# Attention and top-1 mixture of experts on one Trainium2 core: small list copies on another engine, second weight matrix loaded whole, smaller descriptor scratch

## The chip, the cores and the metric

The kernel runs on one core of one Trainium2 chip. The metric is the time of one execution in device microseconds (us); runs are summed up by their median.

## The reference

There is an attention with a sigmoid in place of the softmax, and then a mixture of experts in which each token goes to one expert.

```python
scores = scale * np.matmul(q, k.transpose(0, 1, 3, 2)) - np.log(S)      # 8 x 12 heads, 448 tokens, 64 wide
attn = np.matmul(1.0 / (1.0 + np.exp(-scores)), v)
x = attn laid out as 3584 tokens x 768
logits = x @ w_gate; e_idx = argmax(logits); gate_w = softmax(logits)[e_idx]
eom = sigmoid(x @ w_output_gate)
for e in range(8):
    h = np.maximum(x[mask] @ w1[e], 0.0)      # w1: 768 x 1024
    out[mask] = gate_w * eom[:, e] * (h @ w2[e])      # w2: 1024 x 768
```

## The kernel before, in words

**The stages.** Up to about 269 us the kernel computes the attention on TensorE (PE), writes the token rows to `x_dram` and finds the expert of each token. The mixture follows as a row of *slots*. A slot holds tokens of one expert: 11 full slots of up to 256 tokens (33.3 us each, the first from 272.6 us), then 3 wide slots of up to 192 (27.5 us each, `wide_slot`, from 640.9 us), then 2 half slots of up to 128 (`half_slot`, from 725.3 us to the end). How many of each kind run is read from a table at run time. Every slot after the first full ones stands inside an If on these counts (L1066 full, L1071 wide, L1076 and L1079 half), one nested in the other, so that after the last wide slot one If is not taken and all engines jump out to the half slots.

**One slot.** PE multiplies x by w1 (`layer1`, L623 and L624 in full slots, L797 to L799 in half slots) and the result h by w2 (`layer2`, L648 to L650). Each fp32 operand is split into a rounded high part and a remainder, and three products are added up. The splits are the work of two engines: ScalarE (ACT) writes the high part (L579 for w2 and x, L583 for w1), VectorE (DVE) the remainder (L580, L586). In `half_slot` ACT does, in this order: the high part of w2 rows 0 and 1, then of rows 2 and 3 (both L579), relu of the first half of h (L803), the high part of rows 4 and 5 (L805), a split of h (L579), the high part of rows 6 and 7 (L795), relu of the second half of h (L803). PE's `turn` (L782) transposes each half of h; it comes once in the middle of layer 1 and once after the first part of layer 2.

**What is fetched for the next slots.** GpSimd (POOL) gathers the x rows of the slot after the next, eight transfers per full slot (L545), by the row numbers in a list; DVE transposes them (`turn_x`, L605). SyncE (SP) loads the weights of the next slot as three transfers of w1 and four of w2 (L566), each of two "rows" of 128 x 768 or 128 x 1024 elements. A load is issued only once the engines that read the old content are done.

**The lists.** Row numbers, output rows and gates of a slot are spread from 32 partitions over 128 by small copies, 12 in each of `spread_lists` (L505, L507, L508; five calls) and `spread_two` (L518, L521; two calls), 8 in `spread_rest` (L530, L531; one call): 92 instructions, all on POOL. Before them DVE transposes the list (L501, L513). Two calls lie in the attention (221 and 259 us), one in the second full slot, one in the third, and `spread_two`, two `spread_lists` and `spread_rest` in the fourth one (372.6 to 406.0 us, the code calls it m = EARLY). POOL executes its queue in order: in that slot copies, gathers, the sending of results (L670) and a `drain` (L696) stand in one line.

**w2 in the wide slots.** A wide slot loads only rows 0 to 3 of the next slot's w2 at its end (`load_w2(nx, (0, 2))`). It copies the expert's number and the flag into the tile `held` (L764, DVE). The slot that follows begins with `load_held` (L736 in a wide slot, L770 in the first half slot): SP reads `held` into registers (L539) and issues the loads of rows 4 and 5 and of rows 6 and 7.

Of the kernel before, what the change touches and what calls it, by code (L numbers as in the profile page):

```python
# [42 lines left out]
LATE_F = LATE_MAX + 2  # L43
LATE_N = LATE_F + E + 2
GT = 32
LGR = LATE_N // 4
# [8 lines left out]
def r32(ap):  # L55
    return ap.bitcast(F32)


class Kernel:
# [80 lines left out]
    def constants(self):  # L140
        nc = self.nc
# [64 lines left out]
        own = gl[1].bitcast(I32)  # L206
        a = TS
# [10 lines left out]
        self.ltb = own[:, a:a + 2 * E].rearrange("p (k h w) -> p k h w", h=1, w=2)  # L218
        a += 2 * E
        self.at = own[0:GT, a:a + LGR + 1]  # L220
        a += LGR + 1
        self.held = own[0:1, a:a + 2]

    def row_words(self):
        v, tok = self.nc.vector, self.tok
# [181 lines left out]
    def table_late(self):  # L407
        v = self.nc.vector
# [9 lines left out]
        first = self.tmp_off  # L418
# [61 lines left out]
        v.tensor_copy(self.tab_l[:, 0], both(0)[0:1])  # L480
        v.tensor_copy(self.tab_b, T[0:1, :, 2, 0:E])
        v.tensor_copy(self.tot, end[0:1, :, E - 1])
        v.memset(self.held, 0)
        yield 1

    def take(self, key, tiles):
# [11 lines left out]
    def spread_lists(self, raw, lt, lx):  # L498
        nc, k, g = self.nc, lx.shape[1], lx.shape[2]
        t = self.take("lt32", self.lt32)  # L500
        nc.vector.transpose(t, raw.rearrange("p (t w) -> p w t", w=6))  # L501
        copy = nc.gpsimd.tensor_copy
        for i in range(4):
            r = slice(32 * i, 32 * i + 32)
            copy(lx[r], t[:, i, 0:k * g].rearrange("p (k g) -> p k g", g=g))  # L505
            own = t[:, :, 0:k * g].rearrange("p w (k h q) -> p w k h q", k=k, q=4)
            copy(lt[r, :, :, 0], own[:, 4, :, :, i])  # L507
            copy(r32(lt[r, :, :, 1]), own[:, 5, :, :, i])  # L508

    def spread_two(self, raw, lt, lx):  # L510
        nc, t = self.nc, self.lt32_two
        for j in range(2):
            nc.vector.transpose(t[:, j], raw[:, Q4 * j:Q4 * j + Q4].rearrange("p (t w) -> p w t", w=6))  # L513
        copy = nc.gpsimd.tensor_copy
        two = lambda a: a.rearrange("p (j k) g -> p j k g", j=2)
        for i in range(4):
            r = slice(32 * i, 32 * i + 32)
            copy(two(lx[r]), t[:, :, i].rearrange("p j (k g) -> p j k g", g=8))  # L518
            for w in range(2):
                to = lt[r, :, :, w]  # L520
                copy(two(r32(to) if w else to),  # L521
                     t[:, :, 4 + w].rearrange("p j (k h q) -> p j k h q", h=2, q=4)[:, :, :, :, i])

    def spread_rest(self):
        g = self.nc.gpsimd
        a = EARLY + LATE_F
        for i in range(4):
            r, q = slice(32 * i, 32 * i + 32), slice(32 * (i % 2), 32 * (i % 2) + 32)
            own = self.lts[q, a:, 1]
            g.tensor_scalar(self.ltq[r, :, 0], own[:, :, 0], 2.0, float(i // 2), ALU.mult, ALU.add)  # L530
            g.tensor_copy(r32(self.ltq[r, :, 1]), r32(own[:, :, 1]))  # L531
# [39 lines left out]
    def load_w2(self, s, rows=range(0, 8, 2)):  # L571
        if s is not None:
            self.load_w(s, self.w2, self.w2r, rows)

    def load_held(self):
        self.load_w2(self.slot_regs(self.held.unsqueeze(2), 0, 1), (4, 6))

    def split(self, raw, hi, lo):
        self.nc.scalar.copy(hi, raw)  # L579
# [152 lines left out]

    def wide_slot(self, j, hint):
        cur = self.wide_lists(j)
        if j:
            self.load_held()  # L736
        nx = self.load_slot(self.tab_l, LATE_F + j + 1, self.wide_lists(j + 1))
        self.nc.gpsimd.drain()
        self.split_w2(0)
        for f in range(8):  # L740
            if f == 6:
                self.finish()
            self.layer1(f, n=WS)
            if f == 0:
                hint()
            if f:
                self.high_low(f - 1, HS)
            if f in (1, 3, 5):
                self.split_w2(f // 2 + 1)
        self.high_low(7, HS)  # L750
        self.high_w1(0)
        self.turn_x(nx)
        self.gather(self.wide_lists(j + 2))
        for k in range(3):
            self.split_x(nx, k)
        self.low_w1(0)
        self.split_w1(1)
        self.split_w1(2)
        self.layer2_q(cur, self.ys[0])
        self.load_w2(nx, (0, 2))  # L760
        self.layer2(cur, 0, 0, self.ys[1], self.psy[1])
        self.layer2_due(cur, 0)
        k = LATE_F + j + 1
        self.nc.vector.tensor_copy(self.held, self.tab_l[0:1, 0:3:2, k])  # L764

    def half_slot(self, j, y):
        nc = self.nc
        nx = None
        if j == 0:
            self.load_held()  # L770
        if j + 1 < E:
            nx = self.load_slot(self.tab_b, j + 1, self.half_lists(j + 1))
        if j:
            if nx is not None:
                self.gather(self.half_lists(j + 1))
            nc.gpsimd.drain()  # L776
        (wh, wl), (xh, xl), (hh, hl) = self.w1s, self.xs, self.hs

        def turn(n):
            ps = self.take("x", self.psx).rearrange("p a (b t) -> p (a b) t", b=2)  # L780
            for i in range(4):
                nc.tensor.transpose(ps[:, i], self.hb[:, 128 * (4 * n + i):128 * (4 * n + i + 1)], self.ident)  # L782
            fs = slice(4 * n, 4 * n + 4)
            self.split(ps, hh[:, fs, 0:HS], hl[:, fs, 0:HS])

        w2 = [self.w2_rows(k) for k in range(4)]
        low = lambda k: nc.vector.tensor_tensor(w2[k][2], w2[k][0], r32(w2[k][1]), ALU.subtract)
        for n in range(2):
            c = slice(512 * n, 512 * n + 512)
            ps = self.take("h", self.psh)  # L790
            for d in range(6):
                if n == 1 and d == 3:
                    turn(0)
                    low(2)
                    nc.scalar.copy(w2[3][1], w2[3][0])  # L795
                    low(3)
                nc.tensor.matmul(ps, xh[:, d, 0:HS], wh[d][:, c], start=(d == 0), stop=False)  # L797
                nc.tensor.matmul(ps, xh[:, d, 0:HS], wl[d][:, c], start=False, stop=False)
                nc.tensor.matmul(ps, xl[:, d, 0:HS], wh[d][:, c], start=False, stop=(d == 5))  # L799
            if n == 0:  # L800
                self.split_w2(0)
                self.split_w2(1)
            nc.scalar.activation(self.hb[:, c], ps, AF.Relu)  # L803
            if n == 0:
                nc.scalar.copy(w2[2][1], w2[2][0])  # L805
        cur = dict(lt=self.ltb[:, j])
        pss = self.psy[0:2]
        self.layer2_mm(pss[0], 0, 0, range(2))
        turn(1)
        if j == 0:  # L810
            self.finish()
        if nx is not None:
            self.turn_x(nx)
            self.split_w1(0)
            for k in range(3):
                self.split_x(nx, k)
            self.split_w1(1)
        self.layer2_mm(pss[0], 0, 0, range(2, 4))
        self.layer2_mm(pss[1], 0, 1, range(4))
        self.load_w2(nx)  # L820
        if nx is not None:
            self.split_w1_row(4)
        for n in range(2):
            self.layer2_mm(pss[n], 0, n, range(4, 8))
            self.layer2_out(pss[n], cur, 0, n, y)
        if nx is not None:
            self.split_w1_row(5)
# [296 lines left out]
```

## Time and profile before

| what | us |
|---|---|
| median of 3 runs | 770.81 (770.23 to 771.84) |
| profiled execution, its own time | 771.06 |
| span in its profile | 769.2 |
| mean granted clock of PE in it | 0.997 of full speed |

The profiled execution lies 0.25 us over the median, and its time is 1.9 us more than the span. In the profile a line such as L566 is a line of the kernel; PE is TensorE, PEld its weight load, DVE VectorE, ACT ScalarE, POOL GpSimd, SP SyncE, and a q behind a name is that engine's sequencer. Times in rows are counted from the start of the span. `[1.24 <-DVE due L658]` says that the engine was idle for 1.24 us before the instruction and that the wait was ended by the instruction of DVE on line 658. "x3" is a count of instructions drawn together in one row. PE's matmuls overlap: one starts every 0.17 us (384 columns), 0.23 us (512) or 0.12 us (256), though each lasts longer, so a loss on PE shows as a wider distance between two starts.

### The profile page before, as it was taken

Reading aid. Unit: us, or ns where it says so; the run is one execution under the profiler, and the core shown is the slowest. Engines: PE = TensorE matmul, PEld = TensorE weight load, DVE = VectorE, ACT = ScalarE, POOL = GpSimd, SP = SyncE. Lnnn points to the kernel's source line nnn. Section 1 sums busy time; section 2 is a strip of 40 time slices with the busy share of each in tenths; the row PEclk is TensorE's granted clock in tenths of the full one; section 3 lists DMA queues with packets and bytes.
Section 4 is the critical chain, followed back from the end, with each engine's and each line's share of the span. In section 5 each row is a group of like instructions: output and inputs, shape, how many; then the busy total and the mean of one; then the engine's idle time right before and its main releaser. Section 6 shows DMA issues by size and latency. Waiting matters only on the chain. (4 is left out here: it accounts for less than half of the span.)

```text
span 769.2 us, 15280 instructions
## 1 busy us (share of the span) xinstructions
PE 756.5 (98%) x5823; PEld 581.5 (76%) x5823; DVE 493.9 (64%) x846; ACT 488.4 (63%) x654; POOL 338.0 (44%) x393
## 2 busy tenths in 40 slices
PE   9999999999999999999999999999999999999996
PEld 4457754444434389899998989999899999889785
DVE  3333345435476679967786676858577685887787
ACT  5666656666687756566665565756556574675685
POOL 5000003232154555787885647355372633633522
PEclk9999999999999999999999999999999999999998
DMA  7464544536486340256766497511156755497691
GB/s 257 145 216 138 203 164 146 159 131 217 145 319 246 122 162 1 80 202 221 260 229 225 170 322 287 157 52 41 42 218 212 268 159 215 145 351 255 224 397 47
DMA packets 43790, 145.21 MB, mean 189 GB/s; under 512 B 5671, under 2 KB 7951, under 8 KB 42672
## 3 DMA queue, kind: packets, MB, share of 16 engines
q1 hardware_dynamic: 33872, 119.56, 43.9%
q0 software_dynamic: 9824, 24.46, 9.4%
q8 instruction: 50, 0.82, 0.4%
q14 instruction: 44, 0.36, 0.1%
HBM read 152.61 MB, written 23.06 MB: 228 GB/s over the span
## 5 line engine op out<-in xcount | busy, mean ns | idle before, releaser
L623 PE MATMUL ps<-rounded 128*128 128x512 f32 (+1 forms) x672 | 226.2, 386 | 1.1 <-PEq L1066 0.8
L871 ACT ACTIVATE a<-ps,bias_s 128x896 f32<-128x896 f32 x168 | 169.0, 1008 | 87.1 <-PE ps L869 87.0
L545 POOL DMA_INDIRECT plain<-x_dram,lxs x122 | 180.4, 1479 | 67.9 <-issue 32.2
L869 PE MATMUL ps<-kqv 64*64 64x448 f32 x1344 | 194.3, 542 | 0.0
L878 PE MATMUL ps<-a,kqv 64*64 64x448 f32 x1344 | 192.4, 536 | 0.0
L624 PE MATMUL ps<-rounded 128*128 128x256 f32 (+1 forms) x672 | 184.1, 274 | 1.2 <-DVE due L658 1.2
L648 PE MATMUL ps<-w2h,h 128*128 128x384 f32 x432 | 145.0, 336 | 0.0
L580 DVE TENSOR_TENSOR w2l<-plain,w2h 128x1536 fp32r<-128x1536 f32 x60 | 105.3, 1757 | 61.9 <-ACT w2h L579 61.9
L650 PE MATMUL ps<-w2h,h 128*128 128x384 f32 x432 | 144.5, 334 | 0.0
L649 PE MATMUL ps<-w2l,h 128*128 128x384 f32 x432 | 144.5, 334 | 0.0
L623 PEld LDWEIGHTS ps<-rounded 128*128 128x128 f32 x672 | 125.9, 187 | 24.3 <-issue 2.0
L624 PEld LDWEIGHTS ps<-rounded 128*128 128x128 f32 x672 | 127.3, 189 | 1.6 <-DVE rounded L586 1.6
L869 PEld LDWEIGHTS ps<-kqv 64*64 64x64 f32 x1344 | 66.3, 134 | 67.2 <-issue 52.9
L878 PEld LDWEIGHTS ps<-a,kqv 64*64 64x64 f32 x1344 | 67.5, 133 | 60.8 <-issue 51.9
L586 DVE TENSOR_TENSOR rounded<-plain,rounded 128x2048 fp32r<-128x2048 f32 x46 | 103.4, 2286 | 2.6 <-ACT rounded L583 2.6
L631 ACT COPY gl<-ps 128x256 f32<-128x256 f32 (+1 forms) x112 | 40.4, 361 | 95.3 <-PE ps L624 89.4
L579 ACT CAST w2h<-plain 128x1536 fp32r<-128x1536 f32 x60 | 88.0, 1470 | 16.6 <-PE ps L914 4.8
L583 ACT CAST rounded<-plain 128x2048 fp32r<-128x2048 f32 x46 | 87.2, 1902 | 0.0
L648 PEld LDWEIGHTS ps<-w2h,h 128*128 128x128 f32 x432 | 81.1, 188 | 2.4 <-issue 1.8
L649 PEld LDWEIGHTS ps<-w2l,h 128*128 128x128 f32 x432 | 81.2, 188 | 0.1
L650 PEld LDWEIGHTS ps<-w2h,h 128*128 128x128 f32 x432 | 81.1, 188 | 0.0
L670 POOL DMA_INDIRECT out<-y,due x11 | 18.2, 1651 | 114.2 <-ACT gl L631 92.8
(257 smaller groups left out, 685.0 us busy)
## 6 DMA issues: line engine op xcount, KB each, us to landing
plain<-w SPq DMA_DIRECT2D x68, 768.0 KB
plain<-w SPq DMA_DIRECT2D x48, 1024.0 KB
kqv<-kqv SPq DMA_DIRECT2D x23, 1344.0 KB
x_dram<-xt SPq DMA_DIRECT2D x8, 1344.0 KB
plain<-w SPq DMA_DIRECT2D x6, 512.0 KB
plain<-x_dram,lxs POOLq DMA_INDIRECT x122, 4.3
kqv<-kqv SPq DMA_DIRECT2D x2, 448.0 KB
lst<-plain POOLq DMA_DIRECT2D x1, 726.0 KB, 6.8
```

What stands on the lines that cost most here:

```text
L545: self.nc.gpsimd.indirect_dma_start(out=s["xg"][:, g], out_offset=None, in_=x4, in_offset=bass.IndirectOffsetOnAxis(ap=s["lx"][:, g:g + 1] ...
L579: self.nc.scalar.copy(hi, raw)
L580: self.nc.vector.tensor_tensor(lo, raw, r32(hi), ALU.subtract)
L586: self.nc.vector.tensor_tensor(self.w1p[1][k], self.w1r[:, 2 * k:2 * k + 2], r32(self.w1p[0][k]), ALU.subtract)
L623: nc.tensor.matmul(out, wh[d][:, c], both, start=(d == 0), stop=False)
L624: nc.tensor.matmul(ps[:, 0:n], wl[d][:, c], self.xc[:, d, 0, 0:n], start=False, stop=(d == 5))
L648: nc.tensor.matmul(ps, hh[:, f, tk], wh, start=(f == 0), stop=False)
L649: nc.tensor.matmul(ps, hh[:, f, tk], wl, start=False, stop=False)
L650: nc.tensor.matmul(ps, hl[:, f, tk], wh, start=False, stop=(f == 7))
L869: nc.tensor.matmul(ps[half[h], j, 0:S], kg[half[j], e, 1, o:o + 64], kg[half[j], e, 0], start=True, stop=True)
L871: nc.scalar.activation(at[u % 4], ps[:, :, 0:S], AF.Sigmoid, bias=self.bias_s, scale=1.0 / math.sqrt(D))
L878: nc.tensor.matmul(self.ps_o[e][h][half[j], 0:S], v[half[h], 6 if i == 3 else 3 * e + c, j], a[half[h], j], start=(i in ((0, 3 if h else 4 ...
```

## The change

1. The 92 copies of `spread_lists`, `spread_two` and `spread_rest` are issued on DVE in place of POOL.
2. A wide slot loads all of the next w2 at its end. For rows 4 and 5, and again for rows 6 and 7, DVE first copies one element of the destination onto itself, and the load stands behind this copy. `held`, its two writes and `load_held` go.
3. The scratch for the descriptors of GpSimd's transfers is 8192 in place of 16384 bytes per partition.

```diff
@@ class Kernel
-        a += LGR + 1
-        self.held = own[0:1, a:a + 2]
...
-        v.memset(self.held, 0)
...
     def spread_lists(self, raw, lt, lx):
-        copy = nc.gpsimd.tensor_copy
+        copy = nc.vector.tensor_copy
     def spread_two(self, raw, lt, lx):
-        copy = nc.gpsimd.tensor_copy
+        copy = nc.vector.tensor_copy
     def spread_rest(self):
-        g = self.nc.gpsimd
+        g = self.nc.vector
...
-    def load_held(self):
-        self.load_w2(self.slot_regs(self.held.unsqueeze(2), 0, 1), (4, 6))
...
     def wide_slot(self, j, hint):
         cur = self.wide_lists(j)
-        if j:
-            self.load_held()
...
         self.load_w2(nx, (0, 2))
         self.layer2(cur, 0, 0, self.ys[1], self.psy[1])
         self.layer2_due(cur, 0)
-        k = LATE_F + j + 1
-        self.nc.vector.tensor_copy(self.held, self.tab_l[0:1, 0:3:2, k])
+        for q in (4, 6):
+            first = self.w2r[0:1, q, 0:1]
+            self.nc.vector.tensor_copy(first, first)
+            self.load_w2(nx, (q,))
 
     def half_slot(self, j, y):
-        if j == 0:
-            self.load_held()
...
-    nc = bacc.Bacc("TRN2", target_bir_lowering=False, num_devices=1)
+    nc = bacc.Bacc("TRN2", target_bir_lowering=False, num_devices=1, dynamic_dma_scratch_size=8192)
```

## Rows read from the trace of the kernel before

**Rows 1.** Part 1 of the page: busy time and share of the span of each engine
```profile
PE 756.5 (98%) x5823; PEld 581.5 (76%) x5823; DVE 493.9 (64%) x846; ACT 488.4 (63%) x654; POOL 338.0 (44%) x393
```

**Rows 2.** Waits of PE: waiting line, releaser, us in total, times, longest
```profile
PE ps L624 <- DVE due L658: 1.2, 1, 1.2
...
PE ps L782 <- ACT hb L803: 1.2, 1, 1.2
...
PE ps L797 <- PEq L1071: 0.7, 1, 0.7
PE ps L623 <- DVE gl L632: 0.3, 1, 0.3
```

**Rows 3.** Timeline of PE around 441 us: start, us, instruction, idle before
```profile
440.74 0.40 PE L623 MATMUL ps<-rounded 128*128 128x512 f32 x1
442.37 0.39 PE L624 MATMUL ps<-rounded 128*128 128x256 f32 x1 [1.24 <-DVE due L658]
```

**Rows 4.** Timeline of DVE in the fifth to seventh full slot
```profile
431.35 1.78 DVE L605 STREAM_TRANSPOSE plain<-plain 128x1536 f32<-128x1536 f32 x1 [6.77 <-DMA plain<-x_dram,lxs]
...
442.24 0.15 DVE L658 COPY due<-lts 128x1 int32<-128x1 int32 x1
442.30 0.14 DVE L659 COPY due<-lts 128x1 f32<-128x1 f32 x1
...
492.97 1.78 DVE L605 STREAM_TRANSPOSE plain<-plain 128x1536 f32<-128x1536 f32 x1
```

**Rows 5.** Timeline of POOL in the fourth to sixth full slot
```profile
373.05 1.00 POOL L545 DMA_INDIRECT plain<-x_dram,lxs  x1 [0.15 <-issue]
...
400.73 2.25 POOL L508 COPY lts<-wg 32x8 f32<-32x8 f32 x1
...
416.55 1.04 POOL L545 DMA_INDIRECT plain<-x_dram,lxs  x1 [8.03 <-DVE h L637]
...
461.72 0.98 POOL L545 DMA_INDIRECT plain<-x_dram,lxs  x1 [3.12 <-DVE plain L605]
```

**Rows 6.** Chain that ended last, 723 to 735 us: start, us, what
```profile
723.72 0.28 SPq L539
...
725.61 0.40 SPq L566
...
726.64 7.71 DMA plain<-w
```

**Rows 7.** Timeline of ACT in the first half slot
```profile
724.84 2.86 ACT L579 CAST w2h<-plain 128x1536 fp32r<-128x1536 f32 x2 [3.71 <-PEq L1071]
729.71 0.60 ACT L803 ACTIVATE hb<-ps 128x512 f32<-128x512 f32 x1 [2.01 <-PE ps L799]
730.50 1.48 ACT L805 CAST w2h<-plain 128x1536 fp32r<-128x1536 f32 x1 [0.20 <-DMA plain<-w]
732.24 0.59 ACT L579 CAST h<-ps 128x512 fp32r<-128x512 f32 x1 [0.26 <-PE ps L782]
...
735.81 0.59 ACT L803 ACTIVATE hb<-ps 128x512 f32<-128x512 f32 x1
```

**Rows 8.** Timeline of PE in the first half slot
```profile
731.55 0.60 PE L782 MATMUL ps<-ident,hb 128*128 128x128 f32 x4
...
736.46 0.66 PE L782 MATMUL ps<-ident,hb 128*128 128x128 f32 x4 [1.19 <-ACT hb L803]
```

**Rows 9.** Waits of DVE: waiting line, releaser, us in total, times, longest
```profile
DVE w2l L580 <- ACT w2h L579: 61.9, 50, 5.1
```

**Rows 10.** Part 5, POOL's gathers (busy, mean ns); part 6, their us to landing
```profile
L545 POOL DMA_INDIRECT plain<-x_dram,lxs x122 | 180.4, 1479 | 67.9 <-issue 32.2
...
plain<-x_dram,lxs POOLq DMA_INDIRECT x122, 4.3
```

**Rows 11.** Line 1071 (the If around the wide slots): instructions on SP's sequencer
```profile
L1071 SPq EVENT_SEMAPHORE  x9: 17/17/17, 718.8 to 721.0; - x9
```

**Rows 12.** Waits of SP: waiting line, releaser, us in total, times, longest
```profile
SPq L1071 <- SPq L1071: 6.4, 2, 4.8
```

**Rows 13.** Stretch of the first half slot: busy us of each engine, PE clock, DMA share, GB/s
```profile
731.00:738.00 7.00, 5.81 (x34) 4.95 (x33) 4.29 (x4) 4.33 (x6) 0.00 (x0) 1.00 1.03 414
```

## The prediction

> **What bounds the kernel now.** The first view is the table of busy times: PE is busy for 756.5 of 769.2 us [rows 1]. The other engines stand at 64% or less, so a change pays only where PE waits, and costs only where PE is made to wait. The second view is the list of PE's waits [rows 2], which is short. Three entries lie where this change works: 1.2 us before a matmul of L624, put down to DVE; 1.2 us before `turn` (L782), put down to ACT's relu; 0.7 us at L1071, where the wide slots are left. An entry of 0.3 us at L632 lies beside small DVE work that the change doesn't touch. The change can therefore give back about 2.7 us and no more.
>
> The third view is the timeline around the first entry. Two matmuls that usually start 0.23 us apart start at 440.74 and 442.37 [rows 3]: 1.63 - 0.23 = 1.40 us lost. DVE had finished its last w1 remainder just before L658 at 442.24 [rows 4]. It was late because `turn_x` (L605) waited 6.77 us for gathered x rows and began at 431.35 [rows 4]. In an undisturbed slot L605 comes 20.3 us after the slot's start (492.97, no wait [rows 4], the slot having begun at 472.6), which in the slot from 406.0 would be 426.3. The rows came late because POOL began that slot's gathers at 416.55 [rows 5]; an undisturbed slot begins them 22.4 us after its start (461.72 [rows 5] in the slot from 439.3), here in the slot before, at 372.6 + 22.4 = 395.0. What kept POOL were the list copies, some at 2.25 us each [rows 5], and the drain behind them.
>
> The fourth view is the chain that ended last: it goes through SP's reading of `held` at 723.72, the issues at 725.61 and 726.64, and 7.71 us to the landing of w2 rows 6 and 7 at 734.35 [rows 6]. ACT rounds them, does the second relu at 735.81 [rows 7], and `turn(1)` starts at 736.46 after 1.19 us of PE idle [rows 8]. With the distance of 0.17 us that belongs there, the loss is about 1.36 us.
>
> **Part 1, copies on DVE.** POOL loses 92 instructions; in the slot from 372.6 us it loses 44 (12 + 12 + 12 + 8). Its gathers for the slot after were at 373.05 behind copies [rows 5] and come earlier, and the drain and the next gathers start when `turn_x` has released its buffer, near 395 instead of 416.55. Should the drain alone stay as long as the 8.03 us before those gathers [rows 5], they start near 403, still 13 us ahead of 416.55, where 6.77 us were missing. So the 1.40 us go: **-1.40**. Nothing is late next: L605 then finds its rows and the DVE work behind it moves up by 5 us.
>
> DVE gains the 92. L658 and L659, small copies of the same kind, start 0.06 us apart though each takes 0.15 [rows 4]. So 44 copies cost between 44 x 0.06 = 2.6 and 44 x 0.15 = 6.6 us. Their cover is DVE's wait for ACT before each w2 remainder: 61.9 us in 50 waits, 1.24 us each [rows 9], four of them in the slot, 5.0 us. At 2.6 us the copies cost nothing; at 6.6 us 1.6 us reach layer 2. I take the low end, as the two neighbouring copies are the nearest row: **0** (0 to +1.6). The 12 copies of each of the two slots before (0.7 to 1.8 us) lie under 5.0 us of such waits. In the attention two calls add at most 1.8 us each, and the list of PE's waits has no entry there; they cost nothing.
>
> The low end is what the two rows at 442.24 and 442.30 show [rows 4]. [...]
>
> **Part 2, w2 loaded whole.** Between two wide slots the loads of rows 4 to 7 move ahead by SP's register reads, about 2 us (723.72 to 725.61 [rows 6]); PE waits for none of them there. At the exit from the wide slots more changes. The loads now stand in front of SP's branch at L1071. On leaving, SP brings its semaphores up to the values that the skipped slots would have left: nine semaphore instructions from 718.8 to 721.0 us [rows 11], with 4.8 us of waiting at one point [rows 12], and they end as the last loads issued before them land. ACT's first instruction behind the exit, at 724.84, waits for the sequencers' exit, after 3.71 us of waiting that ends with PE's sequencer at L1071 [rows 7]. Before, SP was through by 721.0 and PE's own exit came last. Now DVE's self-copies end near 723.6 and SP issues rows 4 and 5 at about 723.7 and rows 6 and 7 one us later. From first issue to last landing the same pair took 734.35 - 725.61 = 8.74 us [rows 6], so they land by 732.4. Three w1 loads queued behind that pair before, and now none can, so I take 732.0. SP's remaining semaphores and the hand-over add about 0.4: ACT starts at A = 732.4 instead of 724.84.
>
> What follows A on ACT, by rows 7: two w2 parts 2.86, relu 0.60, third part 1.48, split of h 0.59, fourth part 1.48, relu 0.59, together 7.60; overlapping starts take off about 0.3, so `turn(1)` comes at A + 7.3 = 739.7 instead of 736.46 [rows 8]. `turn(0)`, at 731.55 [rows 8], moves to about A + 3.5 = 735.9, and the 3.5 us of matmuls between the two turns (4.9 us less the 1.36 lost [rows 8]) fit before A + 7.3. **+3.2**, and the old 1.36 us are inside it: this is no longer a wait for w2 rows but for the split of all of them. The lower bound is -1.36, if nothing of ACT waits for SP; the upper is +3.9 (landing 732.4, hand-over 0.7 like PE's at the same exit [rows 2]). I take +3.2, because SP's rows 11 and 12 are the nearest. Behind SP, the first w1 loads of the second half slot start later by some 3 us as everything does: **+0.2** (0 to 0.5).
>
> **Part 3, smaller scratch.** A gather holds POOL 1.48 us and lands after 4.3 [rows 10], so more than two are in flight. No row shows a wait for room. If half the room let only two fly, eight gathers would take 4 x 4.3 = 17.2 us of the 31.3 us between 461.72 and 492.97 [rows 5, 4]: **0**. One at a time would be 34.4 us and 3 us late in each slot; that I give 1 in 100 and leave out.
>
> **Sum.** -1.40 + 0 + 3.2 + 0.2 = +2.0 us on the profiled execution's 771.06, which is 773.06. That execution lies 0.25 us over the median, so 772.8 for the median. A measurement of this kernel can tell about 0.2%, 1.54 us, from no change; the forecast is 0.26% above.
>
> **The rivals.**
> *ACT doesn't wait for SP at the exit.* For it: the releaser that rows 7 name is PE's sequencer, not SP's. Against it: SP was through 3.8 us earlier then, so it could not have been named. The one point that decides is whether ACT's start lies before or after the landing of rows 6 and 7. Then w2 comes 2 us earlier, both losses go, -1.40 - 1.36 = -2.76: 768.05, faster by 0.36%. Chance 0.15.
> *SP waits, but the pair lands sooner.* Nothing is behind the two loads now, and the stretch after them moved 414 GB/s [rows 13]. At that rate the 1.57 MB take 3.8 us. A gather of 0.39 MB lands after 4.3 us [rows 10], so both ends of a transfer take at most 4.3 - 0.9 = 3.4 us. Then the pair lands at 723.7 + 7.2 = 730.9, A is 731.3, `turn(1)` 738.6, +2.1 in place of +3.2. Sum -1.40 + 2.1 + 0.2 = +0.9: 771.4, no change. Against it: the 8.74 us measured for this very pair [rows 6]. Chance 0.17. [...]
> *DVE pays for each copy in full.* As worked out, +1.6 more: 774.4. Chance 0.08.
> *The gap at 441 us stays*, because drain and gathers still end late: +1.4 on the forecast, 774.2. Against it stand the 13 us of room. Chance 0.07.
>
> **How the numbers follow.** The forecast (A from 731.7 to 733.1, 772.1 to 773.5) has 0.53; about a fifth of it lies under 1.54 us. Slower: 0.42 + 0.15 from the two dearer rivals = 0.57. Same: 0.11 + 0.17 = 0.28. Faster: 0.15. The range reaches from 770.1, the quickest form of the second rival, to 774.9, the dearer cases with their own scatter; the first rival and a little at the top lie outside.
>
> **What would show it.** Right: no gap over 0.3 us at 441 us, L605 without a wait near 426, gathers from about 395; SP's semaphore instructions of L1071 ending near 732, ACT's first L579 after the wide slots near 732.4, about 4 us of PE idle before `turn(0)`. Wrong: ACT at 724.8 as now, or the pair landing by 729, or DVE's L637 late against layer 2 between 372 and 406 us.

## The result and the profile after

The changed kernel takes 779.58 us (median of 4 runs, 778.74 to 780.46); the kernel before, on the same chip, 770.52 us. The ratio is 1.0121, 95% interval 1.0094 to 1.0148: 9.1 us slower. The forecast was 772.8 us (770.1 to 774.9): the direction is right, the size is not.

The profiled execution takes 778.74 us, its span is 777.0 us. Its first expert matmul (L617, which is L623 of before) starts at 268.78 us, before at 269.84; the attention ahead of it holds two of the calls whose copies moved, but the kernel before, profiled once more on another chip, also started at 268.32 us, so the 1.1 us say nothing of the change. From there to the end it is 508.2 us against 499.4 us, 8.8 us more, and that is nearly all of the measured difference. So all that follows is read in three stretches of PE's timeline: from the first expert matmul to the first matmul of the half slots (slots), from there to the second transposes, `turn(1)` (exit), and from there to the end (tail).

| | slots | exit | tail | sum |
|---|---|---|---|---|
| before | 455.5 | 11.1 | 32.7 | 499.4 |
| after | 455.9 | 19.3 | 32.9 | 508.2 |

The ends of the exit, first before and then after (before, the second transposes stand in [rows 8] at 736.46):

```profile
725.33 0.47 PE L797 MATMUL ps<-rounded 128*128 128x512 f32 x1 [0.67 <-PEq L1071]
```
```profile
724.70 0.47 PE L789 MATMUL ps<-rounded 128*128 128x512 f32 x1 [0.67 <-PEq L1063]
...
744.04 0.60 PE L774 MATMUL ps<-ident,hb 128*128 128x128 f32 x4
```

PE's waits in the changed kernel (waiting line, releaser, us in total, times, longest; L774 is L782 of before, L617 is L623, L626 is L632, L789 is L797):

```profile
PE ps L774 <- ACT hb L795: 7.2, 1, 7.2
PE ps L617 <- DVE gl L626: 2.1, 3, 1.4
...
PE ps L789 <- PEq L1063: 0.7, 1, 0.7
```

Against [rows 2], the wait for `due` at 441 us is gone, the one for DVE at L626 has grown from 0.3 us once to 2.1 us in three places, and the one of the transposes from 1.2 to 7.2 us, though it is now at the first transposes and no longer at the second. The timeline of PE around them:

```profile
386.74 0.28 PE L618 MATMUL ps<-rounded 128*128 128x256 f32 x1
388.38 0.50 PE L617 MATMUL ps<-rounded 128*128 128x512 f32 x1 [1.37 <-DVE gl L626]
...
738.29 1.11 PE L774 MATMUL ps<-ident,hb 128*128 128x128 f32 x4 [7.21 <-ACT hb L795]
739.05 0.78 PE L789 MATMUL ps<-rounded 128*128 128x512 f32 x1
739.63 0.63 PE L790 MATMUL ps<-rounded 128*128 128x512 f32 x1
740.05 0.63 PE L791 MATMUL ps<-rounded 128*128 128x512 f32 x1
740.48 0.63 PE L789 MATMUL ps<-rounded 128*128 128x512 f32 x1
```

Two things are to be seen. At 386.74 the distance to the next matmul is 1.64 us where 0.12 is usual. And after the long wait the matmuls of 512 columns stand 0.43 us apart, not 0.23. The view by stretches (busy us of each engine, granted PE clock, DMA share, GB/s) says why:

```profile
730.00:738.00 8.00, 1.08 (x5) 0.56 (x3) 1.60 (x1) 3.11 (x3) 0.00 (x0) 0.88 0.17 58
738.00:740.00 2.00, 1.71 (x6) 1.58 (x7) 1.82 (x2) 2.00 (x4) 0.00 (x0) 0.50 0.92 279
740.00:745.00 5.00, 5.00 (x21) 4.28 (x20) 4.02 (x3) 2.33 (x4) 0.00 (x0) 0.71 1.02 419
```

PE idled from 731.1 to 738.3, and in the stretch behind it the granted clock is 0.50 of full speed, where it is 1.00 in [rows 13]. What PE waited for is ACT, and what ACT waited for is SP (timeline of ACT, SP's instructions at the branch, and SP's two last issues):

```profile
734.89 2.84 ACT L573 CAST w2h<-plain 128x1536 fp32r<-128x1536 f32 x2 [14.40 <-SPq L1063]
```
```profile
L1063 SPq EVENT_SEMAPHORE  x9: 17/17/17, 731.0 to 734.7; - x9
```
```profile
723.48 0.37 SPq L563 DMA_DIRECT2D plain<-w  x1
...
724.33 0.37 SPq L563 DMA_DIRECT2D plain<-w  x1
```

In [rows 7] the first split of w2 behind the exit was released by PE's sequencer at 724.84. Now SP is named, with 14.40 us. SP issued rows 4 and 5 at 723.48 and rows 6 and 7 at 724.33, and its semaphore instructions at the branch ended at 734.7. So ACT starts 10.19 us after the first half-slot matmul (724.70) and not 0.49 us ahead of it.

POOL's gathers two slots behind the list copies begin at 395.95 and not at 416.55 [rows 5]; their rows are there when DVE wants them, with no wait, where [rows 4] had one of 6.77 us. First POOL's timeline, then DVE's, with the copies:

```profile
395.95 0.98 POOL L542 DMA_INDIRECT plain<-x_dram,lxs  x1 [16.77 <-DVE plain L599]
```
```profile
380.67 0.17 DVE L502 CAST lxs<-wg 32x32 int32<-32x32 f32 x1
380.76 0.15 DVE L504 CAST lts<-wg 32x8 int32<-32x8 f32 x1
380.84 0.15 DVE L505 COPY lts<-wg 32x8 f32<-32x8 f32 x1
381.00 0.17 DVE L502 CAST lxs<-wg 32x32 int32<-32x32 f32 x1
...
382.03 0.42 DVE L626 TENSOR_TENSOR gl<-gl,ps 128x256 f32<-128x256 f32 x1
...
425.81 1.78 DVE L599 STREAM_TRANSPOSE plain<-plain 128x1536 f32<-128x1536 f32 x1
```

### The profile page after: what moved, and what is told of

It is laid out like the page before. It is cut to its first block, busy times and chain, and to the rows that moved or that the text cites. A ratio compares the mean times of both kernels' runs of the same rounds, so it can differ in the third digit from the quotient of the medians.

```text
span 777.0 us, 15272 instructions
## 1 busy us (share of the span) xinstructions
PE 757.7 (98%) x5823; PEld 594.1 (76%) x5823; DVE 504.1 (65%) x940; ACT 488.4 (63%) x654; POOL 299.4 (39%) x301
## 5 line engine op out<-in xcount | busy, mean ns | idle before, releaser
L617 PE MATMUL ps<-rounded 128*128 128x512 f32 (+1 forms) x672 | 226.2, 386 | 2.8 <-DVE gl L626 2.1
L861 PE MATMUL ps<-kqv 64*64 64x448 f32 x1344 | 168.1, 541 | 0.0
L870 PE MATMUL ps<-a,kqv 64*64 64x448 f32 x1344 | 166.7, 536 | 0.0
L574 DVE TENSOR_TENSOR w2l<-plain,w2h 128x1536 fp32r<-128x1536 f32 x60 | 105.2, 1756 | 72.3 <-ACT w2h L573 72.3
L617 PEld LDWEIGHTS ps<-rounded 128*128 128x128 f32 x672 | 125.8, 187 | 26.4 <-DVE gl L626 3.0
L664 POOL DMA_INDIRECT out<-y,due x11 | 20.0, 1815 | 134.7 <-ACT gl L625 115.1
```

Of the source, the lines that this page charges most:

```text
L574: self.nc.vector.tensor_tensor(lo, raw, r32(hi), ALU.subtract)
L617: nc.tensor.matmul(out, wh[d][:, c], both, start=(d == 0), stop=False)
L861: nc.tensor.matmul(ps[half[h], j, 0:S], kg[half[j], e, 1, o:o + 64], kg[half[j], e, 0], start=True, stop=True)
L870: nc.tensor.matmul(self.ps_o[e][h][half[j], 0:S], v[half[h], 6 if i == 3 else 3 * e + c, j], a[half[h], j], start=(i in ((0, 3 if h else 4 ...
```

## The experiments

All kernels but "three pairs" and "before, once more" were measured on chips slower than the one of the result (the kernel before has medians of 780.3 to 783.1 us there), and their times scatter by several us from execution to execution. So each ratio is to the median of the kernel before on the same chip, and effects of one or two us are read from the stretches of one profiled execution. In this section and in the expectations a pair is one load of two rows of w2; in the prediction "the pair" is both loads, of rows 4 and 5 and of rows 6 and 7.

| kernel | ratio (95%) | slots | exit | tail |
|---|---|---|---|---|
| before, once more | - | 455.2 | 11.1 | 33.0 |
| copies alone | 1.0019 (0.9995 to 1.0042) | 458.2 | 11.4 | 32.5 |
| w2 alone | 1.0106 (1.0071 to 1.0142) | 464.0 | 18.9 | 32.7 |
| scratch alone | 0.9991 (0.9960 to 1.0021) | 457.9 | 11.1 | 32.7 |
| change, PE kept busy | 1.0109 (1.0065 to 1.0153) | 456.2 | 16.7 | 35.9 |
| no self-copy | 1.0012 (0.9985 to 1.0039) | 457.2 | 9.8 | 33.0 |
| copies in layer 2 | 0.9971 (0.9950 to 0.9992) | 453.7 | 11.3 | 33.1 |
| both of these | 0.9987 (0.9962 to 1.0013) | 455.7 | 11.4 | 32.7 |
| change, last pair alone | 1.0038 (1.0012 to 1.0065) | 455.9 | 12.4 | 33.0 |
| change, four gathers | one run | 458.2 | 15.0 | 32.5 |
| three pairs | 0.9986 (0.9967 to 1.0004) | 453.7 | 9.8 | 32.5 |
| three pairs, again | 0.9985 (0.9954 to 1.0017) | 455.6 | 9.8 | 32.5 |

Some slots stretches hold further stalls near the first slots (in "copies alone" distances of 1.92 and 0.84 us in the second slot where 0.61 and 0.12 stand before). "Three pairs, again" has them too and "three pairs", the same kernel, has not, so they come and go without an edit. In this form they stand in three of the nine profiles with the copies on DVE and in none of the others; why is open.

**Copies on DVE alone.**

```diff
-        copy = nc.gpsimd.tensor_copy
+        copy = nc.vector.tensor_copy
```

> Part 1 alone: the list copies on DVE, everything else as before. Theory: the gap of 1.40 us at 441 us goes, but the copies hold back DVE's additions of layer 1 in the fourth full slot, so that PE waits there twice, 0.4 and 1.4 us by idle time, together about 2.0 us by the distances of the matmuls. Net +0.6 us from the first expert matmul (L623 of before) to the end: 500.4 us in place of 499.8; within 0.2% of the kernel before. Rival 1 (the forecast's own term): the copies cost nothing, 498.4 us, 1.4 us faster. Rival 2: what is lost in the whole change comes from the copies, 508 us.

The gap two slots behind the copies is gone and two new distances stand in the fourth slot, 0.78 and 1.72 us where 0.12 is usual: 2.3 us lost, 1.4 won. Without the two longer distances in the second slot the slots take 456.2 us, 0.7 to 0.9 more than the two profiles of before. The ratio holds no change. The theory stands, the two rivals don't.

**w2 alone.**

```diff
-        self.load_w2(self.slot_regs(self.held.unsqueeze(2), 0, 1), (4, 6))
...
+            self.nc.vector.tensor_copy(first, first)
+            self.load_w2(nx, (q,))
```

> Part 2 alone: all of the next w2 loaded at the end of a wide slot behind the self-copies; copies on POOL and the large scratch as before. Theory: all of the loss beyond 1 us is here: SP's semaphore instructions at the exit from the wide slots end with the landing of the last pair, ACT starts 11 us after PE's last matmul of the wide slots, PE idles over 7 us before the first transposes of the half slot and runs at the lower granted clock for some us behind them; +8.2 us, 508.0 us from the first expert matmul to the end, 1.0% to 1.1% slower. Rival: the pair lands late only because of the small scratch or of POOL's changed timing; then ACT starts near 732.4 on the scale of before and the cost is the forecast's +3.2 us, 503.0 us.

ACT's timeline and PE's waits of this kernel:

```profile
749.93 2.85 ACT L573 CAST w2h<-plain 128x1536 fp32r<-128x1536 f32 x2 [14.10 <-SPq L1063]
```
```profile
PE ps L774 <- ACT hb L795: 6.9, 1, 6.9
```

ACT starts 9.9 us after the first half-slot matmul (740.04), and the exit takes 18.9 us, 7.7 to 7.8 more than before. So it comes without the smaller scratch and without the moved copies. (The slots of this run hold stalls at 284 us and in the second and third slot that no other kernel shows so; the sum is therefore not used.)

**Scratch alone.**

```diff
+    nc = bacc.Bacc("TRN2", target_bir_lowering=False, num_devices=1, dynamic_dma_scratch_size=8192)
```

> Part 3 alone: 8192 bytes per partition of descriptor scratch. Theory: nothing, 499.8 us from the first expert matmul to the end, gathers 0.3 us apart on POOL as before, median landing 4.3 us within 0.3. Rival: less room holds the gathers back, seen as waits of POOL before L545 over 0.3 us that no other work explains, and a longer median landing (4.8 us with the whole change).

Ratio 0.9991 around no change. On POOL the gathers follow each other 0.3 us apart; one longer idle time of 4.35 us stands where [rows 5] has 8.03, behind the drain. The slots are 2.4 us longer than on the quicker chip, with small distances of 0.5 to 0.6 us near the router and the first slots and one of 0.98 us some 179 us behind the first expert matmul. The gap that [rows 3] show at 171 us behind it is not there, though the copies are on POOL; in "w2 alone" it is missing too. The median landing isn't in this page. Nothing speaks for a cost, but a fraction of a us can't be excluded.

**The change with PE kept busy in the stall.**

```diff
+                    if j == 0:
+                        for i in range(40):
+                            nc.tensor.matmul(self.psy[1], xh[:, 0, 0:HS], wh[0][:, 0:384], start=(i == 0), stop=(i == 39))
                     turn(0)
```

> The changed kernel with 40 further matmuls of 384 columns (6.9 us) on PE, right before the first transposes of the first half slot, where PE idles; their result is overwritten unread. Theory: the stall is set by ACT's late start, so the added work is free, and it keeps the granted clock at the upper level: the rest of layer 1 behind the transposes runs at 0.23 us per matmul and not 0.43, the second transposes come 1.9 us earlier, 506.8 us from the first expert matmul to the end in place of 508.65. Rival: the slow stretch behind the stall is not the clock's but a wait of its own (weights, w2 splits); then the time stays at 508.6 us, or rises.

The same view by stretches as above, the last two rows being those behind the stall:

```profile
736.00:745.00 9.00, 9.00 (x46) 8.02 (x45) 0.00 (x0) 0.74 (x1) 1.01 (x1) 1.00 0.63 205
745.00:747.00 2.00, 2.00 (x14) 2.00 (x13) 1.23 (x1) 2.00 (x2) 0.00 (x0) 1.00 0.00 0
747.00:752.00 5.00, 5.00 (x29) 4.58 (x28) 4.40 (x4) 4.54 (x6) 0.00 (x0) 1.00 0.93 324
```

And PE's two groups of transposes:

```profile
748.49 0.60 PE L774 MATMUL ps<-ident,hb 128*128 128x128 f32 x4
...
752.05 0.60 PE L774 MATMUL ps<-ident,hb 128*128 128x128 f32 x4
```

The clock stays at 1.00. From `turn(0)` to `turn(1)` it is 3.56 us; in the changed kernel 5.75 (738.29 to 744.04). So 2.2 us of the loss are the clock's. The added matmuls are not quite free: `turn(0)` comes 4.23 us after ACT's start (744.26), in the changed kernel 3.40, which gives 0.8 us back. The exit is 2.6 us shorter, 1.2 of which come from ACT starting earlier in this run. The end was expected 1.9 us earlier and isn't: the tail grew by 3.0 us. There POOL's sending of the first half slot's results met a w2 remainder on DVE and took 5.25 us, where it took 1.47 in the changed kernel, and the last gathers behind it are on the chain that ended last:

```profile
762.35 5.25 POOL L664 DMA_INDIRECT out<-y,gl  x1 [7.27 <-ACT rounded L573]
```

The half-right expectation shows that POOL's last gathers and the splits behind them can set the end of this program: from the start of PE's last matmul to the end it is 10.8 us here, and 7.3 to 7.8 us in all other kernels.

**No self-copy.**

```diff
-        self.load_w2(nx, (0, 2))
+        self.load_w2(nx)
...
-        if j == 0:
-            self.load_held()
```

> The kernel before, but a wide slot loads all four pairs of w2 rows at its end with no self-copy in front and without the held tile; copies on POOL, large scratch. Theory: what costs is a load that is still under way when SP reaches the branch. These four are issued some 13 to 9 us before the first half-slot matmul and land about 3 us before to 1 us after it, so ACT starts within 2 us of that matmul, and PE finds w2 rows 6 and 7 split in time: second transposes 9.8 us after the first half-slot matmul in place of 11.1 before (19.3 in the changed kernel); about 1.4 us faster than before. Rival: with the six gathers in flight the four pairs land no sooner than 4 us after that matmul, ACT is late again, and the second transposes come 12 us after it or later.

The exit is 9.8 us as expected, but the first half-slot matmul itself came late: 2.58 us after the last one of the wide slots, where 1.00 is usual. The branch's rows:

```profile
L1065 SPq EVENT_SEMAPHORE  x9: 17/17/17, 727.6 to 732.1; - x9
...
L1065 ACTq EVENT_SEMAPHORE  x1: 17/17/17, 732.1 to 732.1; - x1
L1065 DVEq EVENT_SEMAPHORE  x1: 21/21/21, 732.2 to 732.2; - x1
```

ACT and DVE leave at 732.1 and 732.2, 2.4 us behind the start of PE's last matmul (729.75); before they leave 0.7 to 0.9 us ahead of it. PE's first half-slot matmul follows at 732.33. SP's own semaphore instructions end at the same time, 732.1; what holds ACT and DVE until then no run shows. 1.3 us won in the exit, 1.6 lost ahead of it: no change.

**Copies in layer 2.**

```diff
             self.spread_two(self.lr_two[1], *at(12, 8))
-            for _ in range(4):
-                yield
-            self.spread_lists(self.lr[5], *at(20, 4))
-            yield
             yield
             self.spread_lists(self.lr[6], self.ltb, self.lxb)
+            for _ in range(9):
+                yield
+            self.spread_lists(self.lr[5], *at(20, 4))
             yield
             self.spread_rest()
```

> Part 1 alone, but the last three groups of copies stand elsewhere in the order: one list in layer 2 of the third full slot, the other and the rest in layer 2 of the fourth, behind DVE's w1 remainders. Theory: the copies cost PE only because they stand ahead of additions that free layer 1's accumulators; in layer 2 DVE idles behind the w1 remainders, so the two waits of 0.4 and 1.4 us in the fourth slot go and the 1.4 us gap two slots later stays away: 1.4 us faster than before, 2.0 us faster than part 1 alone from the first expert matmul to the first half-slot matmul. Rival: the copies cost about as much wherever they stand, since DVE is what ends late in that slot: within 0.5 us of part 1 alone, the waits only moving to the start of the next slot.

What is left in the list of PE's waits of those for DVE at L632:

```profile
PE ps L623 <- DVE gl L632: 0.3, 1, 0.3
```

Both waits of the fourth slot are gone, and so is the gap two slots later. The slots take 453.7 us, 1.5 to 1.8 less than in the two profiles of before. It is the one kernel of the series that is faster than before beyond its interval, 0.9971 (two later kernels with the copies at the same place, at 0.9986 and 0.9985, are not). The copies cost PE by their place, not by their number.

**Both of these.**

> The two edits of the last two kernels together, no smaller scratch. Theory: the effects add up, -1.4 and -1.4 us: 2.8 us, 0.36% faster than before, and PE's only waits in the experts are the two branches and one of 0.3 us. Rival: the end of the program is set by POOL's last gathers and not by PE, and what the half slots win on PE is given back there; then 1.4 us faster.

The edits are those of the last two kernels. Neither came: 0.9987 (0.9962 to 1.0013). PE's first half-slot matmul is 2.97 us behind the last one of the wide slots, and now the granted clock falls as well, so that the exit takes 11.4 us in place of 9.8 (by stretches):

```profile
728.00:732.00 4.00, 1.37 (x8) 1.04 (x8) 0.23 (x3) 0.26 (x1) 2.90 (x3) 1.00 0.55 123
732.00:736.00 4.00, 4.00 (x12) 3.15 (x11) 2.75 (x2) 2.59 (x2) 0.00 (x0) 0.57 0.36 100
```

**The change with the last pair alone behind a self-copy.**

```diff
-        self.load_w2(nx, (0, 2))
+        self.load_w2(nx, (0, 2, 4))
...
-        for q in (4, 6):
+        for q in (6,):
```

> The changed kernel, but of the two late pairs only rows 6 and 7 stay behind a self-copy; rows 4 and 5 are loaded together with rows 0 to 3. Theory: ACT's start follows the landing of the last load by 0.7 us whatever that load is; alone it lands 6 to 8 us after its issue at 1.2 us before the first half-slot matmul in place of 9.9 us after its issue, so ACT starts 5.5 to 7.5 us after that matmul in place of 10.2, and the second transposes come at 13 to 15 us in place of 19.3: 4 to 6 us faster than the changed kernel. Rival: the exit itself takes this long after any late load, by bookkeeping; ACT at 10 us and no gain.

SP's last issue, SP's instructions at the branch, and ACT's timeline:

```profile
731.12 0.37 SPq L563 DMA_DIRECT2D plain<-w  x1
```
```profile
L1063 SPq EVENT_SEMAPHORE  x9: 17/17/17, 736.9 to 737.5; - x9
```
```profile
737.63 2.85 ACT L573 CAST w2h<-plain 128x1536 fp32r<-128x1536 f32 x2 [9.51 <-SPq L1063]
```

Issue at 731.12, SP through at 737.5, ACT at 737.63: 5.3 us after the first half-slot matmul (732.34). All nine of SP's instructions lie within 0.6 us, and ACT follows the last of them again, so the exit has no long bookkeeping of its own. PE's stall is 2.3 us, the clock keeps its level, and the exit takes 12.4 us, even less than the 13 to 15 expected.

**The change with four gathers per wide slot.**

```diff
-        self.gather(self.wide_lists(j + 2))
+        self.gather(self.wide_lists(j + 2), groups=range(4))
```

> The changed kernel, but a wide slot leaves out the last two of its six gathers (the x rows of 64 tokens stay old, so this computes with other rows); in the last wide slot these two are issued at 2.7 and 0.5 us before the first half-slot matmul, beside the two late pairs of w2. Theory: the pairs land 8.6 to 9.9 us after the issue of the second because they share the transfers with these gathers; without them the second lands 7 us or less after its issue, ACT starts 7.5 us or less after the first half-slot matmul in place of 10.2, PE idles 4.5 us in place of 7.2. Rival: the gathers have nothing to do with it, and ACT starts at 9 us or later again.

SP's last issue and ACT's timeline:

```profile
743.35 0.37 SPq L563 DMA_DIRECT2D plain<-w  x1
```
```profile
750.28 2.84 ACT L573 CAST w2h<-plain 128x1536 fp32r<-128x1536 f32 x2 [10.77 <-SPq L1063]
```

The second pair is issued as in the changed kernel (0.38 us before the first half-slot matmul at 743.73), and ACT starts 6.55 us after that matmul. In the three profiles with all six gathers and both late pairs it starts 10.19 us after it (change), 9.89 (w2 alone) and 8.95 (PE kept busy). So leaving out the two gathers beside the pairs is worth 2.4 to 3.6 us. That is one execution, on another chip, and POOL's sending of results, which stands behind the gathers, moves ahead with them: from 0.8 us after that matmul to 2.7 us ahead of it. The two can't be told apart.

**Three pairs early, one held.**

```diff
-        self.load_w2(self.slot_regs(self.held.unsqueeze(2), 0, 1), (4, 6))
+        self.load_w2(self.slot_regs(self.held.unsqueeze(2), 0, 1), (6,))
...
-        self.load_w2(nx, (0, 2))
+        self.load_w2(nx, (0, 2, 4))
```

with the copies in layer 2.

> The copies on DVE with the last three groups in layer 2, and w2 in another split: a wide slot loads rows 0 to 5 at its end, and only rows 6 and 7 are left to the held tile and the slot that follows; large scratch. Theory: three pairs land before the engines leave the wide slots, as in the kernel with the last pair alone, so the exit isn't held; and the one pair left is issued first in the half slot and not second, lands 5 to 6 us after an issue at 0.3 us behind the first half-slot matmul, before ACT wants it at 7.5 us. Second transposes 9.8 us after that matmul in place of 11.1 to 11.3; 1.4 us faster than the kernel with the copies in layer 2 alone, some 3.5 us faster than before (ratio 0.9955). Rival: the third pair loads the transfers ahead of the exit, the jump is late as with all four pairs (2.6 us between the matmuls at the branch in place of 1.0), and nothing is won.

> The kernel before, unchanged, for a profile on the chip of the other runs: 499.4 us within 1.5 us from the first expert matmul to the end, with the gap of 1.6 us between matmuls two slots behind the list copies, and 11.1 us from the first half-slot matmul to the second transposes. Rival: the longer times of this chip come from the experts too; then other gaps show there.

> The kernel with three pairs at the end of a wide slot and the copies in layer 2 once more, for a narrower interval. Theory: 3.4 us less from the first expert matmul to the end, as in its first profile, so a ratio of 0.9955 where nothing else scatters. Rival: the first run's 0.9986 is the true one, and what the profile shows is not in the unprofiled executions.

In the profile of "three pairs" the stretches come out as expected: the exit takes 9.8 us and isn't held, though the one pair left is issued 1.6 us behind the first half-slot matmul and not 0.3. PE's waits in the experts are the two branches and one of 0.3 us:

```profile
PE ps L797 <- DVEq L1070: 0.8, 1, 0.8
PE ps L623 <- PEq L1065: 0.7, 1, 0.7
PE ps L623 <- DVE gl L632: 0.3, 1, 0.3
```

From the first expert matmul to the end it takes 495.9 us, and the kernel before, profiled on the same chip, 499.3 (again with the gap two slots behind the copies and 11.1 us of exit): 3.4 us less. But the medians of the executions, 769.13 and 770.20 us, are 1.1 us apart: 0.9986, where 0.9955 was expected. The second measurement says the same (0.9985; in its profile 497.8 us, with the stalls of the second slot named above). Both intervals hold no change. The executions of "three pairs" fall into a group from 766.7 to 768.1 and one from 770.2 to 771.2 us, and the profiled one is the quickest of the first. What makes the others 3 us longer isn't known.

## Why the prediction was right or wrong

**The gap at 441 us: right.** It was put at -1.40 and is gone, with POOL's gathers beginning at 395.95 (forecast: near 395), L599 at 425.81 without a wait (forecast 426.3). None of the nine profiles with the copies on DVE has it. Of the five with the copies on POOL three have it (1.6 us), "scratch alone" has one of 0.98 us 8 us later, and "w2 alone" has none: it is not in every execution.

**The copies on DVE: wrong step.** "At 2.6 us the copies cost nothing; at 6.6 us 1.6 us reach layer 2." The time of the copies was between the ends: a group of 12 takes 1.36 us (380.67 to 382.03), starts 0.09 us apart within a group of three and 0.16 us to the next, which goes to other partitions. So the rows at 442 us were a fair measure for neighbours, and the rival's count of each copy at its full length was not: 12 x 0.15 to 0.17 would be 1.9 us. What was wrong is the cover. I put the copies under DVE's waits for ACT ahead of the w2 remainders [rows 9], 5.0 us in the slot; but they stand behind a remainder and ahead of the addition (L626) that frees one of layer 1's accumulators, and PE waits for that first. Only 32 of the 44 copies fell into that slot (`spread_two` ran before it, 369.63 to 371.19), they took 3.7 us, less than the 5.0 us of cover, and still PE lost 0.55 and 1.52 us by the distances, 2.1 us in place of 0. "Copies in layer 2" shows that it is the place. The forecast had set aside the entry at L632 in [rows 2] as lying beside work "that the change doesn't touch"; it is the wait at this line that grew from 0.3 to 2.1 us. The rival by which DVE pays for each copy in full had put +1.6, nearer to the 2.1, but for a reason that these rows deny.

**The exit: the mechanism right, the landing too early and the clock left out.** The wait for SP, named at the right instruction, is shown by the row of ACT and by the two kernels in which the landing moves (last pair alone, four gathers). The step put it at +3.2 us; the exit grew by 8.2 (19.3 - 11.1). Of the 5.0 us between them:

- *The landing, +3.1.* The step took 8.74 us from the first issue to the last landing from [rows 6] and then shortened it, since no w1 loads would follow, to 732.0 and A = 732.4, 7.1 us after the first half-slot matmul. Measured: 10.2. The two loads of [rows 6] were issued at 725.61 and 726.64, when POOL had issued its last gather; the changed kernel issues them 2 us earlier, beside the last two gathers. Without these ACT starts 2.4 to 3.6 us earlier (four gathers), enough for most or all of the 3.1. What the loads would collide with ahead of them was not looked at, only what no longer stands behind them.
- *The clock, +1.9.* The forecast had 7.3 us from ACT's start to `turn(1)`; it took 9.15 (734.89 to 744.04), and 7.13 where the clock kept its level (last pair alone, 737.63 to 744.76). The forecast itself gave PE an idle time of about 4 us, and left out the clock behind it: 0.50 behind the 7.2 us of the changed kernel (738 to 740 us), 0.57 behind 3.6 us (four gathers, 753 to 757 us).

The two rivals by which ACT would not wait, or the pair would land sooner, fell: ACT's row names SP. (The second rival's sum of +0.9 is 771.7 us, not 771.4; nothing else hangs on it. Its gather of 0.39 MB is one of 0.098 MB, 128 rows of 192 numbers, by which its 3.4 us for both ends would be 4.1 and its A 732.0, inside the forecast's own 731.7 to 733.1.) The lower end of the range, 770.1, is called the quickest form of that rival; it takes an exit of about +0.5 us (-1.40 + 0.5 + 0.2 = -0.7), a term that no run shows. In the changed kernel SP's semaphore instructions end 11.2 us after the first issue (723.48 to 734.7), even one load alone kept SP for 5.8 us (731.12 to 736.9), and the exit grew by 8.2.

**The scratch: right,** as far as the scatter lets one say.

**The sum.** The +0.2 behind the exit came out (tail 32.7, then 32.9). So -1.40 + 2.1 + 8.2 + 0.2 = +9.1 us, against 8.8 in the profile. The range did not reach that far because both terms went past their dear ends: the copies cost 2.1 where at most 1.6 was allowed, the exit 8.2 where at most 3.9 was. That the forecast still had the sign right rests on the exit alone.

## What to carry to other kernels

Ahead of an If that is left, a load still under way was here a load that others waited for, also ACT, whose first split there wants rows 0 and 1 and not the late ones (it started 10.19 us after the first half-slot matmul, before 0.49 us ahead of it): at such a place count from the issue to the last landing beside all else that is in flight, or issue the load behind the exit. The copies moved to an engine with idle time cost here by what stood right behind them in that engine's order (PE waited 2.1 us for the additions behind them, and the 0.3 us of before once they stood in layer 2); put such work where the next instruction is wanted late. And to a stall of PE add what a lower clock takes from the matmuls behind it: here 2.2 us behind 7.2 us of idle time, and nothing behind 2.3 us (last pair alone).

## What the runs showed of the hardware

- After an idle time of 7.2 us on PE the granted clock fell to 0.50 (738 to 740 us), and after 3.6 us too (four gathers; 0.57 over 753 to 757 us) for a shorter stretch. It fell also after 2.6 us at the branch (both of these; 0.57 over 732 to 736 us), and did not after 2.2 us there (no self-copy; 1.00 over 733 to 736 us). Behind a stall of 2.3 us (last pair alone) it stayed at 1.00:

```profile
741.00:745.00 4.00, 3.97 (x21) 3.32 (x22) 3.71 (x3) 3.70 (x4) 0.00 (x0) 1.00 0.90 359
```

- A sending on POOL that took 1.47 us took 5.25 beside DVE remainders with two inputs (L574, 763.33 to 766.75, PE kept busy), as copies on POOL took 2.25 us beside L586 (396.23 to 402.92, before), where others of the same shape took 0.18.
- With four pairs of w2 loaded ahead of the exit ACT and DVE left it 2.4 us after the start of PE's last matmul (no self-copy), with two 0.9 and 0.7 us ahead of it (before). With three, DVE's exit was what ACT's first split (722.50) and PE's first half-slot matmul waited for, PE 0.8 us (three pairs). Why is not shown.
